# A transformer block on one core: the attention steps, taken apart into units, follow written sequences on all five queues

## The chip, the core and the metric

The kernel runs on one core of a Trainium2 chip. TensorE (PE, with its weight loads shown as PEld), VectorE (DVE), ScalarE (ACT) and GpSimd (POOL) compute; the fifth queue, SyncE (SP), issues the transfers. Each has an instruction queue of its own, which runs in the order in which it was written, and semaphores hold an instruction until its data are there and its buffer is free. The metric is the device time of one execution in microseconds, the median of several runs.

## The reference

One transformer block over 2048 tokens of width 1024, all in float32. `phi` is t + 1 for positive t and exp(t) otherwise.

```python
mod = silu(c) @ w_mod                           # six rows of 1024: sa, ca, ga, sb, cb, gb
h = layernorm(x) * (1 + ca) + sa
# attention: 32 heads of 32, four segments of 512 tokens
for s in range(4):
    p = softmax(qs @ ks.T * scale + mask)       # the mask is -1e9 * (row < col)
    o = g * (phi(qs) @ M) / (phi(qs) @ z + 1e-6) + (1 - g) * (p @ vs)
    M += phi(ks).T @ vs;  z += sum(phi(ks))     # the memory, used by the next segment
x = x + ga * (concat(o) @ wo)
h = layernorm(x) * (1 + cb) + sb
x = x + gb * ((gelu(h @ w_gate) * (h @ w_up)) @ w_down)     # the feed-forward is 3584 wide
```

## The kernel before

**Products.** Almost every product is made of three: each operand is cut into a high part, of the type float32r, and a low part, the rest. ACT or DVE writes the high part (a cast or a copy), DVE or POOL the low one (a subtraction), and PE multiplies high by high, low by high and high by low.

**Stages.** The opening loads x and the conditioning, normalises segments 0 and 1 and projects the first group. Then come 32 attention steps: a step is one group of four heads (there are eight) in one segment; the first sixteen steps are segments 0 and 1 of each group, the others segments 2 and 3. Then the output projection, and the feed-forward, which is most of the time. The change lies in the attention steps alone.

**An attention step.** In the loop's turn n, three steps overlap: the projections of step n+1, the scores of step n and the values of step n−1.

- K and Q: 96 key-value matmuls (128x256, in two PSUM banks, tag `mm`) and 24 query matmuls (128x512). ACT and DVE copy them out (`kn`, `vx`); PE transposes `kn` (`kT`); ACT and DVE cut kT and q into high and low (`kh`, `kl`, `qh`, `ql`), and SP spreads these over the rows of `ks` and `qs`.
- S: for each of four rows of score blocks, four matmuls (one per head) into PSUM banks of the tag `s`, of which there are five. DVE adds the mask and takes the row maximum (`mm`) in one instruction; ACT takes the exponential of the result (`sj`, three buffers) for its sum (`ll`) alone. From `mm` DVE makes `mt`, turns it (`tt`) and writes it into rows 96 to 127 of `qs`, so that the transposed scores come out with the maximum subtracted; from `ll` come `rc` (DVE) and `rx` (ACT).
- T and O: the transposed scores of the step before (`T`, four column blocks, 16 matmuls, again banks of the tag `s`), the exponential on ACT (`pt`), the causal edge on POOL, and the product with `vx` (`O`, 32 small matmuls). T needs the `qs` rows from the step's own maxima.
- A (`sums`) adds to the memory `M`; M (`memory`) makes `mz`, the matmuls `num`, the denominators `dn` and the share `ry`. R and Y transpose the factors `rx` and `ry`, and DVE combines them with O; SP stores the result.

Beside these, each pair of steps loads and cuts the three weights of the next group (POOL subtracts in quarters), steps 1 to 9 normalise segments 2 and 3 (rows `na`: statistics, scale, eight transposes and their scaling, a store to `hT_d`), one or two columns of the conditioning are made in each step by a 1024-wide DVE reduction (`wm`), steps 14 and 15 load `hT_d` back and cut it, and steps 29 to 32 prepare the output projection. Weights, rows of x and conditioning columns share four buffers (tag `raw`).

**What sets the order.** PE's order is written: the string `ORDER` of 30 letters says which generator is advanced next, and `todo` holds the loads and cuts with their positions. The same string serves every step. PE follows the program order. On SP, DVE, ACT and POOL a scheduler places the attention's instructions by its own estimates, a few excepted (`hold`); in the opening and the feed-forward these queues follow the program too.

Of the kernel before, what the change touches and what calls it, by code (L numbers as in the profile page):

```python
# [19 lines left out]
P = 128  # L20
# [16 lines left out]
def block_kernel(ctx: ExitStack, tc: tile.TileContext, x, c, wmod, wq, wkv, wo, beta, wg, wu, wd, out):  # L37
# [149 lines left out]
    def load_hT(src, s, dst, name, late=False):  # L187

        rs = []
        for k in range(KT // 2 + 1):  # L190
            if k < KT // 2:
                r = raw_tile(f"r{name}_{k}").rearrange("p (k t) -> p k t", t=L)
                nc.sync.dma_start(r, src[2 * k * P:(2 * k + 2) * P, s * L:(s + 1) * L].rearrange("(k p) t -> p k t", p=P))
                rs.append(r)
            yield
            for q in range(2 if k > 0 else 0):
                r = rs[k - 1]
                hi = hT_tile(f"hh{name}_{k}_{q}", s)
                lo = hT_tile(f"hl{name}_{k}_{q}", s)
                if late:  # L200
                    nc.scalar.activation(hi, r[:, q], AF.Copy)
                else:
                    nc.vector.tensor_copy(hi, r[:, q])
                (nc.gpsimd if q else nc.vector).tensor_sub(lo, r[:, q], f32(hi))
                dst.append((hi, lo))
                yield
# [20 lines left out]
    def norm_tiles(src, dst, segs, jscale, jshift, name, tiles=range(4), wait=0, get=raw_tile, more=[]):  # L227
# [8 lines left out]
        def stats(q):  # L236
            t = xs[q]
            mv, rs = norm_stats([t[:, :L], t[:, L:]], f"{name}{toks[q]}", name == "a")
            norm_scale([t], mv, rs, f"{name}{toks[q]}")

        def turn(q, h):
# [6 lines left out]
            for k in range(4):  # L248
# [3 lines left out]
                if name == "b" and k % 2:  # L252
# [4 lines left out]
            if wait:  # L257
                later(3, send_h)
            else:
                send_h()  # L260

        if wait:
            for q in range(len(toks)):
# [10 lines left out]
                for h in range(2):  # L274
                    turn(q, h)
                    yield
            return
        if name == "a":
            load(0)
            yield  # L280
            for q in range(len(toks) + 1):
                if q < len(toks):
                    stats(q)
                yield
                for h in range(2):
# [53 lines left out]
    hT, W, Mst, ST, SC, PK = {}, {}, {}, {}, {}, {}  # L339
# [5 lines left out]
    def weights(half, g, at):  # L345

        W[g] = [None] * 3
        raws = [None] * 3

        def get(i):  # L350
            raws[i] = fetch((wq[g], wkv[g, 0], wkv[g, 1])[i], f"{i}_{half}_{g}")

        def cut(i):
            W[g][i] = split_w(raws[i], wsp_tile(f"w{i}_{half}_{g}"))

        for pos, f, i in at:
            todo.append((pos, lambda f=f, i=i: (get, cut)[f](i)))
# [14 lines left out]
    def kv_tiles(n, nm):  # L372
# [3 lines left out]
        ST[n] = [None, ks_t[n % 2], vx, None]  # L376
# [7 lines left out]
    def k_out(n, s, nm, kn, vx):  # L384
        ks = ks_t[n % 2]
        ps = s_ps("kT" + nm)
        for t in range(4):
            nc.tensor.transpose(ps[:, t * P:(t + 1) * P], kn[:, t], ident)  # L388
        kh = t2("kh" + nm, "sp", bufs=4, dt=F32R)
        kl = t2("kl" + nm, "sp", bufs=4, dt=F32R)  # L390
        nc.scalar.activation(kh, ps, AF.Copy)
        nc.vector.tensor_sub(kl, ps, f32(kh))
        for qd, srct in ((0, kh), (1, kh), (2, kl)):
            nc.sync.dma_start(f32(ks[qd:96:3]), f32(srct))
        if s < NSEG - 1:
            knf = kn.rearrange("p a b -> p (a b)")
            e = tmp_tile("ek" + nm)
            nc.scalar.activation(e, knf, AF.Exp)
            nc.vector.tensor_scalar_min(e, e, 1.0)
            pk = t2("pk" + nm, "pk", shape=(P, 4, P))  # L400
            nc.vector.scalar_tensor_tensor(pk.rearrange("p a b -> p (a b)"), knf, 0.0, e, op0=ALU.max, op1=ALU.add)
            PK[n] = pk, vx

    def q_out(n, s, nm, ps):
        qh = t2("qh" + nm, "sp", bufs=4, dt=F32R)
        ql = t2("ql" + nm, "sp" if n else "sj", bufs=4 if n else 3, dt=F32R)
        nc.scalar.activation(qh, ps, AF.Copy, scale=SCALE)
        nc.vector.scalar_tensor_tensor(ql, ps, SCALE, f32(qh), op0=ALU.mult, op1=ALU.subtract)
        qs = t2("qs" + nm, "qs", bufs=2, dt=F32R, shape=(P, 4, L))
        pq = None  # L410
        if s > 0:
            e = tmp_tile("eq" + nm)
            nc.scalar.activation(e, ps, AF.Exp)
            nc.vector.tensor_scalar_min(e, e, 1.0)
            pq = t2("pq" + nm, "pq", bufs=2)
            nc.vector.scalar_tensor_tensor(pq, ps, 0.0, e, op0=ALU.max, op1=ALU.add)
        for qd, srct in ((0, qh), (1, ql), (2, qh)):
            nc.sync.dma_start(f32(qs[qd:96:3]), f32(srct))
        ST[n][0], ST[n][3] = qs, pq

    def kv_part(n, g, s):

        nm = f"{g}_{s}"
        kn, vx = kv_tiles(n, nm)
        for tp in range(2):
            ps = mm_ps(f"kv{nm}_{tp}")
            for t in range(2):
                for kt in range(KT):
                    kv_mm(ps[:, 2 * P * t:2 * P * (t + 1)], g, s, 2 * tp + t, kt)
                    if kt == 3 or (kt == 7 and t == 0):  # L430
                        yield
            kv_out(ps, kn, vx, 2 * tp, 2)
            yield
        k_out(n, s, nm, kn, vx)
        yield

    def q_part(n, g, s):

        nm = f"{g}_{s}"
        ps = mm_ps("q" + nm)  # L440
        for kt in range(KT):
            q_mm(ps, g, s, kt)
            if kt % 2 == 1 and kt < KT - 1:
                yield
        q_out(n, s, nm, ps)
        yield

    def first_part(n, g, s):

        nm = f"{g}_{s}"  # L450
        kn, vx = kv_tiles(n, nm)
        kv = [mm_ps(f"kv{nm}_{tp}") for tp in range(2)]
        psq = o_ps("q" + nm)
        for kt in range(KT):
# [14 lines left out]
        k_out(n, s, nm, kn, vx)  # L469
        q_out(n, s, nm, psq)  # L470
        yield

    def sums(n, g, s):

        nm = f"{g}_{s}"
        if s < NSEG - 1:
            pk, vx = PK.pop(n)
            ps = s_ps("M" + nm)
            for t in range(4):
                nc.tensor.matmul(ps[:, :P + 2], pk[:, t], vx[:, t], start=(t == 0), stop=(t == 3))  # L480
            M = t2("Mt" + nm, "M", bufs=11, shape=(P, P + 2))
            if s == 0:
                nc.vector.tensor_copy(M, ps[:, :P + 2])
            else:
                nc.vector.tensor_add(M, ps[:, :P + 2], Mst[g, s - 1])
            Mst[g, s] = M
        yield

    def scores(n, g, s):
        nm = f"{g}_{s}"  # L490
        qs, ks, vx, pq = ST[n]
        mm = t2("mm" + nm, "mm", bufs=2, shape=(P, 4, 4))
        ll = t2("ll" + nm, "ll", bufs=2, shape=(P, 4, 4))

        for i in range(4):
# [10 lines left out]
            if i < 3:  # L506
                yield

        mt = t2("mt" + nm, "mt", bufs=2, dt=F32R, shape=(P, 4, 4, 2))
        nc.vector.tensor_copy(mt[:, :, :, 0], mm)  # L510
        nc.vector.tensor_sub(mt[:, :, :, 1], mm, f32(mt[:, :, :, 0]))
        tt = t2("tt" + nm, "tt", bufs=1, shape=(P, P))
        mtf = f32(mt.rearrange("p a b c -> p (a b c)"))
        for a in range(4):
            nc.vector.transpose(tt[96:128, 32 * a:32 * a + 32], mtf[32 * a:32 * a + 32])
        for i in range(4):
            nc.vector.tensor_scalar(qs[96:128, :, i * P:(i + 1) * P], tt[96:128].unsqueeze(1).to_broadcast([32, 4, P]),  # L517
                                    seli[96:128, i:i + 1], None, op0=ALU.mult)

        rc = t2("rc" + nm, "rc", bufs=2, shape=(P, 4, 4))  # L520
        nc.vector.reciprocal(rc, ll)
        nc.vector.tensor_mul(rc, rc, omg[:, 4 * g:4 * g + 4].unsqueeze(1).to_broadcast([P, 4, 4]))
        rx = t2("rx" + nm, "rx", shape=(P, 4, 4, DH))
        nc.scalar.activation(rx, rc.unsqueeze(3).to_broadcast([P, 4, 4, DH]), AF.Copy)
        SC[n] = [rx, None]

    def memory(n, g, s):
        nm = f"{g}_{s}"
        pq = ST[n][3]
        if s > 0:  # L530
            M = Mst[g, s - 1]
            mz = t2("mz" + nm, "mz", bufs=1, shape=(P, P + 4))
# [15 lines left out]
            SC[n][1] = ry  # L548
        yield

    def values(n, g, s):
        nm = f"{g}_{s}"
        qs, ks, vx, pq = ST.pop(n)
        rx, ry = SC.pop(n)

        po = o_ps("O" + nm)
        pts = {}
# [13 lines left out]
        def PV(kc):  # L571
            for j in range(4):
                nc.tensor.matmul(po[32 * j:32 * j + 32, kc * P:], vx[:, kc, 32 * j:32 * j + 32], pts[kc, j],  # L573
# [984 lines left out]
```

## Time and profile before

| | |
|---|---|
| median of 3 runs | 2793.05 us (2791.14 to 2793.16) |
| the profiled execution | 2794.09 us |
| its span, first to last instruction | 2792.4 us |
| mean granted TensorE clock | 0.995 |
| PE busy | 2737.9 us, 98% of the span |
| DVE, ACT, POOL busy | 1553.5, 1202.4, 880.2 us |

The profile belongs to one execution. Matmuls are pipelined and overlap in the records, and the end of one is modelled; so PE can look busy while it waits, and the distance from one matmul's start to the next is the safer reading. "Idle before" a group names the instruction that ended the wait.

### The profile page before, as it was taken

To read this page: it belongs to the slowest core of one execution; us is meant where nothing else is said; L and a number is where in the kernel's file an instruction comes from. 1 tells how busy PE (TensorE), PEld (TensorE's weight loads), DVE (VectorE), ACT (ScalarE), POOL (GpSimd) and SP (SyncE) were. 2 spreads that over 40 slices of the span, in tenths; PEclk is the share of its full clock that TensorE was granted. 3 is DMA by queue.
4 is the path that set the end of the run, shared out by engine and by line. 5 is a ranking of instruction groups with operands and counts; after the bars stand their busy time and mean duration, and the time that the engine had idled before them with its cause. 6 is when DMAs were issued, how large, how long until landed. Compare 5 with 4: busy or idle time off the path is not lost.

```text
span 2792.4 us, 43055 instructions
## 1 busy us (share of the span) xinstructions
PE 2737.9 (98%) x14748; PEld 2285.7 (82%) x14748; DVE 1553.5 (56%) x3499; ACT 1202.4 (43%) x2826; POOL 880.2 (32%) x1424
## 2 busy tenths in 40 slices
PE   7999999999999999999999999999999999999999
PEld 6888888888888777778888878888888888888887
DVE  7666566866666735555555445344343245475456
ACT  5777776767676624234332333111111033233323
POOL 5333334433332523245555552535352000000000
PEclk8999999999999999999999999999999999999999
DMA  6455544454434538768898767999999687796563
GB/s 229 138 136 145 148 118 137 137 147 114 125 99 118 153 123 264 260 257 309 309 357 312 279 266 276 344 353 367 353 360 332 225 288 266 261 306 217 177 205 127
DMA packets 244890, 637.77 MB, mean 228 GB/s; under 512 B 24768, under 2 KB 49344, under 8 KB 244672
## 3 DMA queue, kind: packets, MB, share of 16 engines
q1 hardware_dynamic: 244672, 635.03, 67.5%
q8 instruction: 116, 1.90, 0.3%
q14 instruction: 102, 0.84, 0.1%
HBM read 372.79 MB, written 211.81 MB: 209 GB/s over the span
## 4 chain that ended last, share of the span: by engine, by line
PE 84%; DVE 5%; ACT 5%; issue 2%; DMA 2%; POOL 2%; SPq 0%; ACTq 0%; DVEq 0%; POOLq 0%
PE f L1049 36%; PE y L1248 19%; PE kv L364 10%; PE y L633 4%; PE q L370 4%; PE T L564 3%; PE O L573 2%; PE S L500 2%; ACT sj L504 2%; ACT pt L566 1%; POOL w L181 1%; ACT w L176 1%; DVE qs L517 1%; PE num L538 0%; PE M L480 0%
## 5 line engine op out<-in xcount | busy, mean ns | idle before, releaser
L1049 PE MATMUL f<-A,B 128*128 128x512 f32 x4704 | 1075.0, 390 | 3.4 <-DVE c L1069 1.6
L1049 PEld LDWEIGHTS f<-A,B 128*128 128x128 f32 x4704 | 880.8, 188 | 190.7 <-DVE c L1069 2.8
L1248 PE MATMUL y<-B,L 128*128 128x512 f32 x2352 | 533.3, 389 | 0.0
L1248 PEld LDWEIGHTS y<-B,L 128*128 128x128 f32 x2352 | 441.4, 188 | 91.7
L502 DVE CUSTOM_DVE_ANT_0 sj<-S,mask 128x384 f32<-128x384 f32 (+3 forms) x512 | 231.0, 487 | 213.6 <-PE S L500 178.4
L504 ACT ACTIVATE sj<-sj,mm 128x384 f32<-128x384 f32 (+3 forms) x512 | 280.9, 551 | 47.1 <-DVE mm L502 46.6
L567 POOL TENSOR_SCALAR_AFFINE_SELECT pt<-pt 128x128 f32<-128x128 f32 x512 | 164.2, 340 | 347.9 <-ACT pt L566 340.3
L566 ACT ACTIVATE pt<-T 128x256 f32<-128x256 f32 (+3 forms) x512 | 180.7, 456 | 99.2 <-PE T L564 93.4
L763 ACT ACTIVATE L<-X 128x512 fp32r<-128x512 f32 x168 | 105.8, 630 | 256.4 <-PE y L1248 165.8
L364 PE MATMUL kv<-w,hhh 128*128 128x256 f32 x1024 | 201.4, 285 | 0.0
L765 DVE TENSOR_TENSOR L<-X,L 128x512 fp32r<-128x512 f32 x168 | 115.8, 690 | 144.6 <-ACT L L763 144.5
L181 POOL TENSOR_TENSOR w<-r,w 128x256 fp32r<-128x256 f32 x180 | 130.7, 757 | 162.9 <-ACT w L176 152.6
L1072 ACT ACTIVATE g<-g 128x512 f32<-128x512 f32 x56 | 35.3, 631 | 340.0 <-DVE g L1071 340.0
L364 PE MATMUL kv<-w,hha 128*128 128x256 f32 x896 | 175.5, 284 | 0.2 <-DVE vx L382 0.2
L988 POOL TENSOR_TENSOR rw<-rw,gbb 128x256 f32<-128x256 f32 x112 | 92.0, 855 | 247.1 <-DMA rw<-wd 187.2
L364 PEld LDWEIGHTS kv<-w,hhh 128*128 128x128 f32 x1024 | 166.5, 192 | 0.5
L364 PEld LDWEIGHTS kv<-w,hha 128*128 128x128 f32 x896 | 144.9, 191 | 1.2 <-PE kT L388 0.4
L364 PE MATMUL kv<-w,hlh 128*128 128x256 f32 x512 | 145.1, 283 | 0.0
L564 PE MATMUL T<-qs,ks 128*128 128x256 f32 (+2 forms) x512 | 121.3, 346 | 12.1 <-ACT pt L566 6.7
L633 PE MATMUL y<-wo,hho 128*128 128x512 f32 x384 | 128.2, 398 | 1.9 <-DVE xr L637 1.9
L364 PE MATMUL kv<-w,hla 128*128 128x256 f32 x448 | 126.6, 283 | 0.0
L1065 ACT ACTIVATE g<-f 128x512 f32<-128x512 f32 x56 | 33.5, 598 | 207.3 <-PE f L1049 207.3
(242 smaller groups left out, 4213.3 us busy)
## 6 DMA issues: line engine op xcount, KB each, us to landing
bc_d<-B SPq DMA_DIRECT2D x189, 512.0 KB, 5.3
B<-bc_d SPq DMA_DIRECT2D x189, 512.0 KB, 5.5
B<-wc_d SPq DMA_DIRECT2D x112, 512.0 KB, 3.7
hid_d<-g SPq DMA_DIRECT2D x56, 512.0 KB, 4.5
wc_d<-T SPq DMA_DIRECT2D x56, 512.0 KB, 7.3
X<-hid_d SPq DMA_DIRECT2D x112, 256.0 KB, 4.7
wr<-gd_d SPq DMA_DIRECT2D x84, 256.0 KB, 4.1
ks<-kh SPq DMA_DIRECT2D x64, 256.0 KB, 4.5
```

Of the source, the lines that this page charges most:

```text
L181: eng.tensor_sub(w[:, 1, k:k + 256], r[:, k:k + 256], f32(w[:, 0, k:k + 256]))
L364: nc.tensor.matmul(ps, b[:, sl], w[:, a], start=(kt == 0 and a == 0 and b is hi), stop=(kt == KT - 1 and a == 1), **kw)
L370: nc.tensor.matmul(ps, w[:, a], b, start=(kt == 0 and a == 0 and b is hi), stop=(kt == KT - 1 and a == 1), **kw)
L502: nc.vector.tensor_tensor_reduce(out=sj[:, :nv], in0=ps[:, :nv], in1=mask[:, L - nv:], scale=-1.0, scalar=3.4e38, op0=ALU.add, op1=ALU.min ...
L504: nc.scalar.activation(sj[:, :nv], sj[:, :nv], AF.Exp, bias=mm[:, j, i:i + 1], scale=-1.0, accum_out=ll[:, i, j:j + 1])
L564: nc.tensor.matmul(ps[:, :nn], ks[:, j, kc * P:(kc + 1) * P], qs[:, j, L - nn:], start=True, stop=True)
L566: nc.scalar.activation(pt, ps[:, nn - n:nn], AF.Exp)
L567: nc.gpsimd.affine_select(pt[:, :P], pt[:, :P], pattern=[[1, P]], compare_op=ALU.is_ge, fill=0.0, base=0, channel_multiplier=-1)
L633: nc.tensor.matmul(ps, b[:, i * P:(i + 1) * P], w[:, a, g % 2], start=(g == 0 and a == 0 and b is hi), stop=(g == G - 1 and a == 1))
L765: eng.tensor_sub(lo[:, k], src[:, k], f32(hi)[:, k])
L1049: nc.tensor.matmul(ps, B[m, i][:, a, kt * P:(kt + 1) * P], A[p, i, kt][b], start=(start and kt == 0 and a == 0 and b == 0), stop=(kt == 3 ...
L1248: nc.tensor.matmul(banks[t], ops[k][:, y, t * P:(t + 1) * P], B[slots[k]][:, x], start=(i not in (2, 4, 3) and j == 0 and x == 0 and y == ...
```

## The change

The loop with its string and its `todo` list is replaced by `attention()`. Each step's work is cut into some seventy named units, and `ORDER` gives for each kind of step the sequence in which they are written: the step's number or numbers are the key. PE's order thus changes too, and SP, DVE, ACT and POOL follow the same written sequence, without the scheduler. A unit is what one function writes, on whatever engines: `S0` to `S3` the rows of scores, `T0` to `T3` and `P0`, `P2` the values, `K0` to `K7` and `Q0` to `Q3` the projections (12 and 6 matmuls each), `o0`, `o1` their copies, `kt`, `ek`, `dk`, `qo`, `ea`, `eb`, `dq` what follows them, `tm`, `tq`, `tr` the maxima and shares, `A`, `mz`, `nu`, `dn` the memory, `rt`, `rm`, `yt`, `zs` the end of the values, `G`, `C`, `D`, `l`, `L`, `m` the weights' load, high part and low halves, `ns`, `nc`, `n0`, `n1`, `nd`, `ne`, `nl` the norm's statistics, scale, turns, stores and load, `wl`, `wd` the conditioning's load and reduction, `x` a piece of loading, `ga`, `wo`, `wp` the output projection's.

Besides, in the norm the second four scalings of a row go from ACT to DVE; in `load_hT` the high part of every second column goes to ACT and POOL subtracts its low part in two halves; the stores of the first output rows to `x1_d` are put off by two steps. The matmuls are the same.

```diff
-    ORDER = "K N K V K V N K K V N V K V K S Q S V V S K A S Q M K Q Q V V"
-    ORDER0 = "K N K N K N K N K K S K S K S K S A K K M"
+    ORDER = {
+        (0,):
+            "K N K G1 N K N K G2 N G0 K K S0 K S1 C1 K S2 l1 K C2 S3 L1 l2 tm tq A tr L2 K",
+        (1,):
+            "T0 K0 K1 D0 ns K2 T1 rt nc P0 mz m0 nu dn K3 T2 n0 n1 o0 Q0 Q1 T3 nd S0 ne nl m1 P2 S1 rm S2 K4 "
+            "Q2 S3 yt tm Q3 K5 K6 K7 tq wl qo o1 zs tr dq A kt ea eb dk ek",
+        (2, 4, 6, 8):
+            "G1 Q0 T0 wd Q1 T1 Q2 P0 ns nc T2 Q3 T3 qo G2 n0 rt P2 K0 ea eb S0 C1 K1 dq S1 K2 S2 l1 K3 n1 K4 "
+            "nl C2 S3 L1 rm l2 K5 tm G0 wl K6 o0 K7 nd o1 ne tr A tq yt kt dk L2 ek zs",
+        (3, 5, 7):
+            "ns D0 K0 K1 T0 K2 T1 nc m0 K3 wl o0 wd P0 n0 K4 S0 K5 S1 mz Q0 S2 Q1 A S3 nd K6 m1 n1 tm nl Q2 "
+            "tq rt T2 Q3 ne T3 qo ea K7 P2 o1 rm nu dq tr dn yt kt dk eb zs ek",
...
+        (18, 20, 22, 24, 26, 28):
+            "G2 G0 K0 K1 K2 T0 K3 T1 G1 o0 rt P0 T2 Q0 T3 S0 Q1 S1 mz wd Q2 Q3 qo C1 K4 C2 S2 K5 S3 P2 rm l1 "
+            "dq ea yt zs eb K6 K7 A tm nu l2 o1 kt tr ek wl dk tq L1 L2 dn",
+        (19, 21, 23, 25, 27):
+            "mz wd D0 K0 K1 K2 m0 m1 K3 o0 T0 K4 T1 Q0 S0 K5 S1 Q1 rt S2 P0 S3 Q2 T2 tm K6 Q3 T3 wl tq qo K7 "
+            "P2 rm o1 nu ea kt yt tr dq dn dk zs wd ek wl eb",
...
+    def attention(nseg1):
+        load, stat, scale, turn, put = norm_tiles(x, hT_d, (2, 3), 1, 0, "a")
...
+        for n in range(len(steps) + 1):
+            u = {}
+            if n > 0:
+                values(u, n - 1, *steps[n - 1][1:])
+            if n < len(steps):
+                scores(u, n, *steps[n][1:])
...
+            elif n + 1 < len(steps):
+                project_in(u, n + 1, *steps[n + 1][1:])
...
+            for q in next(o for k, o in ORDER.items() if n in k).split():
+                beside(u, q, n)
+        send(True)
+        waiting[0] = False
...
-        free_order[0] = True
...
+        with tc.manual_schedule(engines={E.SP, E.DVE, E.Activation, E.Pool}):
+            attention(nseg1)
```

What this does to the queues, at the two places of which the prediction speaks most. First the beginning of step 1: PE from the memory's matmuls on (M, then the transposes kT, then the projections kv and the first T). Before:

```order
L480 MATMUL M_0_945<-vx_0_306,pk_0_629 128x130 x4
L388 MATMUL kT_1_952<-ident,kn_1_665 128x128 x4
L364 MATMUL kv_0_0_991<-w_0_1_878,hha_0_252 128x256
L364 MATMUL kv_0_0_991<-w_0_1_878,hla_0_253 128x256
...
L364 MATMUL kv_0_0_991<-w_0_1_982,hla_7_544 128x256
L564 MATMUL T_0_00_1028<-qs_0_635,ks_111 128x512
L564 MATMUL T_0_10_1033<-qs_0_635,ks_111 128x512
```

and now:

```order
L566 MATMUL M_0_948<-vx_0_306,pk_0_629 128x130 x4
L401 MATMUL kT_1_962<-ident,kn_1_667 128x128 x4
L615 MATMUL T_0_00_992<-qs_0_635,ks_111 128x512
L615 MATMUL T_0_10_997<-qs_0_635,ks_111 128x512
L615 MATMUL T_0_20_1002<-qs_0_635,ks_111 128x512
L615 MATMUL T_0_30_1007<-qs_0_635,ks_111 128x512
L367 MATMUL kv_0_0_1015<-w_0_1_867,hha_0_252 128x256
```

The 24 kv matmuls that stood between kT and the first T now stand behind it. On DVE, what T waits for (the copies of vx, the memory's copy Mt, the maxima mt, their turn tt, the rows of qs), before:

```order
L382 COPY vx_1_666<-kv_1_1_669 128x2x128
L502 ISA sj_0_33_925,mm_0_806<-S_0_33_923,mask 128x512
L502 ISA mm_0_806 128x1
L483 COPY Mt_0_950<-M_0_945 128x130
L510 CAST mt_0_928<-mm_0_806 128x16
L533 TENSOR_TENSOR mz_1_1340<-Mt_0_950,blk 128x128
L511 TENSOR_TENSOR mt_0_928<-mm_0_806,mt_0_928 128x16
L534 TENSOR_SCALAR mz_1_1340<-sel_106,Mt_0_950 128x4
L515 STREAM_TRANSPOSE tt_0_931<-mt_0_928 32x32 x4
L521 RECIPROCAL rc_0_940<-ll_0_807 128x16
L517 TENSOR_SCALAR qs_0_635<-tt_0_931,seli 32x4x128 x4
```

and now:

```order
L526 ISA sj_0_33_929,mm_0_810<-S_0_33_927,mask 128x512
L526 ISA mm_0_810 128x1
L534 CAST mt_0_936<-mm_0_810 128x16
L535 TENSOR_TENSOR mt_0_936<-mm_0_810,mt_0_936 128x16
L539 STREAM_TRANSPOSE tt_0_939<-mt_0_936 32x32 x4
L543 TENSOR_SCALAR qs_0_635<-tt_0_939,seli 32x4x128 x4
L569 COPY Mt_0_953<-M_0_948 128x130
```

The memory's copy, mz and rc went behind the rows of qs. Second, SP where the weights of a later group are loaded, in step 6 (r are weights, wm a conditioning column, R an output to be stored, na a row of x for the norm). Before:

```order
L155 DMA wm_2978<-wmod 128x1024
L111 DMA r_0_4_3180<-wkv 128x1024
L598 DMA oT_d<-R_0_2970 128x512
L111 DMA r_0_4_3239<-wkv 128x1024
L394 DMA ks_111<-kh_0_3086 32x4x512 x2
L394 DMA ks_111<-kl_0_3087 32x4x512
```

and now:

```order
L654 DMA oT_d<-R_0_3021 128x512
L111 DMA r_0_4_3143<-wkv 128x1024
L111 DMA r_0_4_3278<-wkv 128x1024
L390 DMA qs_1_3277<-qh_1_3271 32x4x512 x2
L390 DMA qs_1_3277<-ql_1_3272 32x4x512
L238 DMA na_3452<-x 128x1024
L111 DMA r_0_4_3501<-wq 128x1024
```

The two key-value weights now stand side by side behind the store; before, the store stood between them.

More of the change, by code (lines that the diff above doesn't have):

```diff
@@ L382, in kv_out, with spread, after_kv @@
         nc.vector.tensor_copy(vx[:, t:t + n, :P], psv[:, :, P:])
-    def k_out(n, s, nm, kn, vx):
+    def spread(dst, parts):
+        for row, part in parts:
+            nc.sync.dma_start(f32(dst[row:96:3]), f32(part))
+    def after_kv(u, n, s, nm, get):
         ks = ks_t[n % 2]
[L386 to L402, printed above, removed]
@@ L437, in q_part, with turned @@
[L437 to L446, printed above, removed]
+        tiles = {}
+        def turned():
+            kn = get()[0]
+            ps = s_ps("kT" + nm)
+            for t in range(4):
+                nc.tensor.transpose(ps[:, t * P:(t + 1) * P], kn[:, t], ident)
+            kh = tiles["h"] = t2("kh" + nm, "sp", bufs=4, dt=F32R)
+            kl = tiles["l"] = t2("kl" + nm, "sp", bufs=4, dt=F32R)
+            nc.scalar.activation(kh, ps, AF.Copy)
+            nc.vector.tensor_sub(kl, ps, f32(kh))
@@ L525, in scores, with maxima @@
[L525 to L530, printed above, removed]
+        def maxima():
+            mm = d["mm"]
+            mt = t2("mt" + nm, "mt", bufs=2, dt=F32R, shape=(P, 4, 4, 2))
+            nc.vector.tensor_copy(mt[:, :, :, 0], mm)
+            nc.vector.tensor_sub(mt[:, :, :, 1], mm, f32(mt[:, :, :, 0]))
+            tt = d["tt"] = t2("tt" + nm, "tt", bufs=1, shape=(P, P))
+            mtf = f32(mt.rearrange("p a b c -> p (a b c)"))
+            for a in range(4):
+                nc.vector.transpose(tt[96:128, 32 * a:32 * a + 32], mtf[32 * a:32 * a + 32])
```

440 lines of the change are left out of this document (259 added, 181 removed).

## The prediction

> **What bounds the kernel now.** I read the shares of the page first, then the stages, then pairs of attention steps.
>
> The page's busy line, and its chain of waits:
>
> ```profile
> PE 2737.9 (98%) x14748; PEld 2285.7 (82%) x14748; DVE 1553.5 (56%) x3499; ACT 1202.4 (43%) x2826; POOL 880.2 (32%) x1424
> ...
> PE 84%; DVE 5%; ACT 5%; issue 2%; DMA 2%; POOL 2%; SPq 0%; ACTq 0%; DVEq 0%; POOLq 0%
> ```
>
> TensorE sets the end. A shorter time must come from its waits, and the change removes no matmul. Now the stages (columns: stretch, its length, then busy us and instructions of PE, PEld, DVE, ACT, POOL, then granted clock, DMA share, GB/s):
>
> ```profile
> 95.50:997.20 901.70, 885.21 (x6417) 758.47 (x6420) 608.10 (x2002) 639.24 (x1844) 324.04 (x736) 1.00 0.47 130
> ...
> 1172.00:2255.00 1083.00, 1078.18 (x4771) 888.39 (x4771) 497.24 (x709) 278.40 (x493) 454.00 (x556) 1.00 0.85 311
> ```
>
> The change leaves the feed-forward alone (the second row is its first part, with 4.8 us of idle PE). It acts on the first row, the attention steps 1 to 31, and on a few us at either side. Cut at the first O matmul of a step, that row is:
>
> ```profile
> 95.50:155.40 59.90, 58.76 (x429) 49.84 (x431) 38.94 (x129) 44.54 (x124) 20.71 (x48) 1.00 0.48 120
> 155.40:275.40 120.00, 118.03 (x861) 101.02 (x864) 78.39 (x258) 92.87 (x265) 39.10 (x97) 1.00 0.52 142
> 275.40:337.90 62.50, 59.52 (x432) 50.54 (x435) 38.67 (x125) 47.71 (x138) 21.76 (x52) 1.00 0.51 138
> 337.90:395.40 57.50, 56.22 (x421) 48.71 (x424) 35.45 (x120) 41.20 (x119) 21.85 (x50) 1.00 0.51 142
> 395.40:450.20 54.80, 54.80 (x417) 48.25 (x420) 33.37 (x119) 37.65 (x112) 12.82 (x38) 1.00 0.38 104
> 450.20:568.00 117.80, 114.65 (x836) 97.44 (x838) 87.99 (x274) 77.93 (x228) 51.15 (x100) 1.00 0.52 152
> 568.00:681.20 113.20, 111.55 (x837) 97.21 (x840) 77.04 (x269) 80.28 (x230) 43.12 (x100) 1.00 0.49 131
> 681.20:848.70 167.50, 167.35 (x1252) 145.78 (x1256) 110.56 (x381) 116.77 (x342) 55.39 (x138) 1.00 0.41 115
> 848.70:903.90 55.20, 55.20 (x421) 48.70 (x423) 35.15 (x127) 37.29 (x112) 12.63 (x38) 1.00 0.37 104
> 903.90:997.20 93.30, 89.14 (x553) 71.00 (x556) 72.56 (x202) 63.00 (x176) 45.49 (x76) 0.98 0.47 139
> ```
>
> Two pairs of steps, 54.80 and 55.20 us, have PE busy to the last tenth. They are the **floor** that the trace itself shows: the first for the first half of the steps, the second for the later half, which has one numerator group and one Y transpose more and one M group less. Steps 1 to 8 also transpose the normalised rows, in groups of four:
>
> ```profile
> 303.49 0.66 PE tpa L247 x4
> ...
> 308.95 0.59 PE tpa L247 x4
> ```
>
> That is 0.63 us a group, so 1.9 us for three groups in a pair and 2.5 for four.
>
> **The room.** Row by row, length less floor: 59.9 − 56.7 = 3.2; 120.0 − 114.6 = 5.4; 62.5 − 57.3 = 5.2; 57.5 − 56.7 = 0.8; then 0; 117.8 − 110.5 = 7.3 (the second of its pairs is given 0.9 more for one more numerator group); 113.2 − 110.4 = 2.8; 167.5 − 165.6 = 1.9; 0; and 93.3 − 82.7 = 10.6 (three steps, 1.5 pairs). In the last step two more waits stand:
>
> ```profile
> 997.14 3.30 PE L573 MATMUL O<-pt,vx 128*32 128x512 f32 x16
> ...
> 1007.62 0.41 PE L573 MATMUL O<-pt,vx 128*32 128x128 f32 x2 [1.16 <-POOL pt L567]
> ```
>
> The same 16 O matmuls take 1.64 us elsewhere (row below), so 1.6 + 1.2 = 2.8. In all **40 us**: 14.6 in steps 1 to 8, 12.0 in the middle, 13.4 at the end.
>
> ```profile
> 681.20 1.64 PE O L573 x16
> ```
>
> How this room is read matters. Span less PE busy gives only 901.7 − 885.2 = 16.5 us. The weight loads give another answer: they fill 758.47 of 901.70 us, 84.1%, against 48.25 of 54.80, 88.0%, in the dense pair; 901.7 × (1 − 84.1/88.0) = 40. [...]
>
> **What makes the room now.** At one of the longest stalls, SP and ACT show it (SP's sequencer first):
>
> ```profile
> 288.04 0.33 SPq L598 DMA_DIRECT2D oT_d<-R  x1
> 293.53 0.33 SPq L111 DMA_DIRECT2D r<-wkv  x1
> ...
> 299.43 1.06 ACT L176 ACTIVATE w<-r 128x1024 fp32r<-128x1024 f32 x1 [4.99 <-DMA r<-wkv]
> 300.39 0.61 ACT L524 ACTIVATE rx<-rc 128x512 f32<-128x512 f32 x1
> ...
> 304.89 1.24 ACT L225 ACTIVATE na<-na,mra,rsa 128x1024 f32<-128x1024 f32 x1 [1.46 <-DVE mra L223]
> ```
>
> A weight load stands in SP's queue behind an output store that is itself late. ACT's queue has the weight's cut at its head and stands still for 5 us, then for 1.5 us more at the norm scale. The exponentials that T needs are behind both. The whole stage:
>
> ```profile
> ACT rx L524 <- DVE rc L522: 52.9, 28, 4.0
> ...
> ACT w L176 <- DMA r<-wkv: 19.7, 6, 5.0
> ...
> ACT na L225 <- DVE mra L223: 10.4, 8, 2.0
> ```
>
> **The change, part by part.** (1) *Loads.* G1 and G2 open an even step, side by side on SP, and their cuts C1 and C2 come behind S0 and S2: at least ten units of PE, some 12 us, against the 5 us lost above. I count the 19.7 us of ACT waiting as gone. (2) *Norm.* The statistics (ns) and the scale (nc) are parted by T0 to T1 in odd steps; in even steps they are still adjacent, so part of the 1.46 us waits stays, on DVE instead of ACT. (3) *S rows.* The written order puts a K unit of 12 matmuls between S rows in steps 2 to 8. One K unit is 1.44 us:
>
> ```profile
> 683.51 1.44 PE kv L364 x12
> ...
> L504 ACT ACTIVATE sj<-sj,mm 128x512 f32<-128x512 f32 x124 | 87.9, 713 | 0.5
> L504 ACT ACTIVATE sj<-sj,mm 128x384 f32<-128x384 f32 x124 | 74.5, 604 | 0.0
> ```
>
> Four exponentials take 4 × 604 ns = 2.4 us for S2 and 2.9 for S3; between these two PE has K3, a group of transposes and K4, 1.4 + 0.6 + 1.4 = 3.4. ACT keeps up, and the banks come free in time. (4) *Moved work.* Half of the norm's transposed scalings (32 of 64, 378 ns by the row below) go from ACT to DVE, 1.5 us in each of eight steps; eight casts of the hT load in steps 14 and 15 go from DVE to ACT, 8 × 0.62 = 5.0 us off a DVE that is busy 88.0 of 117.8. Both land on engines with at least 7 us free in a step, so 0. (5) *POOL's halves* of a 512-wide subtraction, 2 × 757 ns against 1416: 0.1 us each, under DVE and PE work, 0.
>
> ```profile
> L255 ACT ACTIVATE hta<-tpa,modT 128x128 f32<-128x128 f32 x64 | 24.2, 469 | 5.1 <-PE tpa L247 5.1
> ...
> L203 DVE CAST hhh<-rh 128x512 fp32r<-128x512 f32 x16 | 9.7, 619 | 0.0
> ...
> L204 POOL TENSOR_TENSOR hlh<-rh,hhh 128x512 fp32r<-128x512 f32 x8 | 11.3, 1416 | 3.2 <-DVE hhh L203 2.8 <-issue 0.4
> ...
> L181 POOL TENSOR_TENSOR w<-r,w 128x256 fp32r<-128x256 f32 x180 | 130.7, 757 | 162.9 <-ACT w L176 152.6 <-PE S L500 6.7 <-DVE mm L502 3.5
> ```
>
> (6) *The first step loses.* T0 now follows kT at once; before, 24 kv matmuls lay between.
>
> ```profile
> 88.91 1.19 PE L564 MATMUL T<-qs,ks 128*128 128x512 f32 x4 [1.40 <-DVE qs L517]
> ...
> 85.13 0.29 DVE L483 COPY Mt<-M 128x130 f32<-128x130 f32 x1
> ...
> 87.17 1.69 DVE L517 TENSOR_SCALAR qs<-tt,seli 32x512 fp32r<-32x512 f32 x4
> ```
>
> DVE is clear of S at 85.13 and now makes mt, tt and qs without the M copy, mz and rc between them: qs ends near 88.2 instead of 88.9. But kT is done at 84.2, so PE stands still for 4.0 us where it stood for 1.4 with 2.9 us of kv done. Net loss 2 us. A stall of this kind has a second price:
>
> ```profile
> 55.00:60.00 5.00, 2.43 (x20) 2.19 (x19) 4.90 (x9) 3.85 (x7) 1.59 (x2) 0.99 0.55 149
> 60.00:65.00 5.00, 5.00 (x27) 4.56 (x27) 2.29 (x5) 0.78 (x1) 2.96 (x4) 0.67 0.83 169
> ```
>
> After 2.6 us of idleness the clock was 0.67 for 5 us: 1.7 us lost. I take 3 us in all for step 1, between 2 (no throttle) and 5 (throttle, and P0 late too). [...]
>
> **The sum.** Left over after the change: the first pair 3.2 + 3 = 6.2; for the 26 steps between, 0.3 us each (what the regular pairs at 681 to 848 show: 1.9 us in six steps), 8; at the end 4 of 13.4, since DVE has 72.6 us of work in what would be 82.7 us. That is 18 of 40, a gain of **22 us**. Bounds: 40 if all reaches the floor (and step 1 costs nothing), 0 if 1.25 us a step stays. The profiled execution took 2794.09 us, 1.0 over the median; 2794 − 22 = 2772 for it, 2771 for the median. I say **2771**.
>
> **The rivals.** (a) *Only idle PE can be won.* If busy PE hides nothing, the room is 16.5 + 2.8 = 19.3 us, less the 3 and 8 above: 8 won, 2785. For it: 98% busy. Against it: the two dense pairs. (b) *The stalls move.* In a written queue one late unit delays all behind it; if four fifths of the 26.6 us in steps 1 to 28 come back elsewhere and the end keeps its 13.4, 5 us are won: 2788. For it: in steps 3 to 6 ACT is busy 77% and DVE 65% of the time, in bursts. (c) *Slower: late work ahead of T0.* The tr unit has a fixed place before kt and ek; ACT waits there for DVE's rc, and behind it stand kh, ek and T0's exponentials. The present price is 52.9/28 = 1.9 us a wait. If T0 or its exponentials were late by that in each of 30 steps, 57 us are added to a floor 40 below: 2810. It decides from 40/32 = 1.25 us a step on. Against it, in step 2, as counted from row means:
>
> ```profile
> L502 DVE CUSTOM_DVE_ANT_0 sj<-S,mask 128x512 f32<-128x512 f32 x128 | 84.2, 685 | 7.1 <-ACT sj L504 4.3 <-PE S L500 0.7
> ```
>
> After S3, DVE owes four such reductions (2.7), the R product, tm, two copies of vx, rc and M (some 3.5 together by their means) and qs (1.7), 7.9 us; PE has K5, K6, K7, K0, K1 (7.2) and M, Y, kT (some 1.8) ahead of the next T0, 9.0 us. T0 has 1 us to spare: enough, though little. (d) *Nothing moves*: the late half is dense already, and the early half is bound by data that come no sooner in another order: 2793. For it: the pair at 395 shows that the old order can be dense. Against it: the same pair shows that data can be in time.
>
> **How the numbers follow.** Forecast 0.60 (2753 to 2781); (a) 0.16; (b) and (d) together 0.11, on either side of where a gain begins to show; (c) 0.13. A difference under 0.2%, 5.6 us, cannot be told from none. Faster: 0.60 + 0.16 + 0.02 of (b) = 0.78; same: the other 0.09, and 0.01 of a mild (c); slower 0.12. The range from 2753 to 2791 takes in (a) and (b), and leaves out (c) and a little at the low end.
>
> **What would show it.** Right: the cut of the second key-value weight no longer waits for its load; pairs in steps 3 to 8 take 57 to 58 us; the three regular pairs stay at 55 to 56; the first T waits about 4 us for qs; the last three steps take 86 us instead of 93. Wrong: T's wait for pt or qs in most steps, ACT standing at rx, or the pairs at 681 to 848 growing past 57 us; then rival (c) has it.

## The result, and the profile after

The changed kernel takes 2774.22 us (median of 4 runs, 2772.03 to 2775.41); beside it the kernel before took 2792.10 us (2790.61 to 2793.16). The ratio is 0.9935, 95% interval 0.9918 to 0.9953: 17.9 us faster, where 22 were forecast. The profiled execution took 2774.08 us (20.0 less than before), its span is 2772.4 us. The busy line and the chain of waits of the page:

```profile
PE 2725.8 (98%) x14748; PEld 2286.4 (82%) x14748; DVE 1568.4 (57%) x3519; ACT 1204.0 (43%) x2806; POOL 888.9 (32%) x1448
...
PE 89%; DVE 4%; issue 2%; POOL 2%; DMA 1%; ACT 1%; SPq 0%; POOLq 0%; ACTq 0%; DVEq 0%
```

PE's part of the chain grew from 84% to 89%, ACT's fell from 5% to 1%. The stages, cut at the same O matmuls as before (columns as there), then the feed-forward's stretch:

```profile
98.67:157.59 58.92, 58.82 (x438) 51.46 (x437) 39.88 (x135) 45.29 (x128) 19.28 (x49) 1.00 0.55 159
157.59:270.72 113.13, 113.13 (x857) 100.23 (x857) 82.55 (x274) 89.03 (x249) 41.54 (x97) 1.00 0.53 150
270.72:327.30 56.58, 56.58 (x429) 50.12 (x429) 40.56 (x134) 44.38 (x124) 23.24 (x53) 1.00 0.48 132
...
671.12:838.87 167.75, 167.75 (x1249) 146.18 (x1248) 116.98 (x391) 118.34 (x343) 56.54 (x138) 1.00 0.44 123
...
891.54:977.85 86.31, 83.59 (x540) 68.52 (x539) 62.70 (x186) 60.91 (x169) 39.42 (x78) 0.98 0.46 137
98.67:977.85 879.18, 875.79 (x6432) 761.03 (x6431) 615.05 (x2020) 639.30 (x1825) 329.73 (x753) 1.00 0.46 133
1172.00:2255.00 1083.00, 1078.06 (x4771) 888.32 (x4770) 501.25 (x713) 280.05 (x496) 445.16 (x546) 1.00 0.86 314
```

The whole stretch of steps 1 to 31 fell from 901.70 to 879.18 us, although 24 key-value matmuls came into it from the start. Steps 3 to 6 fell from 120.00 to 113.13, steps 7 and 8 from 62.50 to 56.58; the regular pairs (167.50, now 167.75) and the feed-forward did not move. Weight loads now fill 761.03/879.18 = 86.6% of the stretch, before 84.1%, in the dense pair 88.0%.

Steps are cut differently now (some projections moved to a neighbour), so I also take, for every matmul, the distance to the next one's start less the usual distance of its kind (the 30th percentile in the kernel before; for O a mean). The sum over a stretch is time lost by PE, in us, whatever stands in it. "Start" is the first M matmul to the first O; "last" runs from the O of step 32 to the first feed-forward matmul. Where a kernel is told below by its place, it is by this table:

| kernel | start | 1–8 | 9–12 | 13–16 | 17–27 | 28–31 | last |
|---|---|---|---|---|---|---|---|
| before | 3.2 | 20.0 | 3.9 | 9.0 | 9.0 | 12.6 | 14.1 |
| changed | 8.5 | 4.9 | 2.0 | 5.6 | 7.9 | 10.2 | 12.4 |
| old order, written queues | 13.3 | 90.4 | 32.1 | 42.2 | 123.5 | 69.7 | 15.6 |
| new order, scheduler | 11.0 | 25.2 | 6.1 | 8.6 | 8.9 | 9.5 | 9.1 |
| POOL alone by scheduler | 8.7 | 6.8 | 3.8 | 7.4 | 8.0 | 9.1 | 17.2 |
| S rows together | 9.7 | 26.3 | 2.0 | 5.6 | 8.0 | 10.5 | 12.5 |
| load twice | 8.7 | 8.8 | 2.0 | 5.6 | 7.8 | 10.2 | 12.4 |
| three operations back | 8.8 | 8.5 | 2.0 | 11.4 | 7.8 | 11.2 | 11.9 |
| halves back | 9.8 | 4.8 | 2.0 | 8.1 | 7.8 | 12.0 | 12.8 |
| T0 later | 6.5 | 6.5 | 2.0 | 5.6 | 8.0 | 11.5 | 15.3 |
| end mended | 9.7 | 4.9 | 2.0 | 5.6 | 8.0 | 8.3 | 9.5 |
| both | 6.5 | 6.5 | 2.0 | 5.6 | 8.0 | 8.0 | 9.8 |

The change won 15.1 in steps 1 to 8, 5.3 in 9 to 16, 1.1 in 17 to 27, 4.1 at the end, and lost 5.3 at the start: 20.3, as much as the 20.0 us between the two profiled executions.

### The profile page after: what moved, and what is told of

Same layout as the page of the kernel before. It is cut to its first block, busy times and chain, and to the rows that moved or that the text cites. A ratio compares the mean times of both kernels' runs of the same rounds, so it can differ in the third digit from the quotient of the medians.

```text
span 2772.4 us, 43014 instructions
## 1 busy us (share of the span) xinstructions
PE 2725.8 (98%) x14748; PEld 2286.4 (82%) x14748; DVE 1568.4 (57%) x3519; ACT 1204.0 (43%) x2806; POOL 888.9 (32%) x1448
## 4 chain that ended last, share of the span: by engine, by line
PE 89%; DVE 4%; issue 2%; POOL 2%; DMA 1%; ACT 1%; SPq 0%; POOLq 0%; ACTq 0%; DVEq 0%
PE f L1107 35%; PE y L1306 19%; PE kv L367 12%; PE q L373 6%; PE y L690 4%; PE S L524 3%; PE T L615 3%; PE O L627 3%; PE num L583 1%; PE M L566 1%; PE tpb L250 0%; POOL t L827 0%; PE R L633 0%; PE kT L401 0%; PE kv L496 0%
## 5 line engine op out<-in xcount | busy, mean ns | idle before, releaser
L615 PE MATMUL T<-qs,ks 128*128 128x256 f32 (+2 forms) x512 | 108.3, 334 | 7.5 <-DVE qs L543 4.6
```

The source lines that it names most:

```text
L615: nc.tensor.matmul(ps[:, :nn], ks[:, j, kc * P:(kc + 1) * P], qs[:, j, L - nn:], start=True, stop=True)
```

## The experiments

Each is compared with the kernel before, run beside it; differences to the changed kernel are differences of medians. The kernel before took 2792.1 to 2794.5 us beside the different runs, so a difference of some 2 us between medians decides nothing by itself. The table is finer: where an edit touches nothing, its rows agree to 0.2 us in steps 1 to 27, but they differ by 1 us at the start and by up to 3 us from step 28 on.

**The order alone, and the written queues alone.** The new order with the scheduler on the other queues:

```diff
-        with tc.manual_schedule(engines={E.SP, E.DVE, E.Activation, E.Pool}):
-            attention(nseg1)
+        free_order[0] = True
+        attention(nseg1)
```

> The changed kernel with its sequence of units, PE still in that sequence, but with the scheduler placing the instructions of SP, DVE, ACT and POOL in the attention, as in the kernel before. Theory (the gain is the new order of units, which moves stalls out of steps 1 to 16 on PE): most of the gain stays, 2774 to 2784. Rival (the gain is that the queues are written rather than scheduled): it goes, 2788 to 2800.

Measured 2801.31 us, ratio 1.0028 (1.0016 to 1.0039): slower than before. And the old order of 30 letters, written out for all queues (the old loop inside the `manual_schedule` of the changed kernel):

> The kernel before with its old string of 30 letters, but SP, DVE, ACT and POOL follow the program in the attention too, without the scheduler. Theory (order of units): nothing is won; the old generators write long pieces at once, so that late work stands ahead of urgent work: 2793 to 2830. Rival (written queues are the gain): under 2783.

Measured 3110.88 us, ratio 1.1142 (1.1126 to 1.1159). PE's longest sums of waits in the attention part (us in total, times, longest), with the scheduler:

```profile
PE T L615 <- DVE qs L543: 7.9, 1, 7.9
PE O L627 <- POOL pt L618: 6.4, 9, 1.2
```

and with the old order:

```profile
PE num L538 <- DVE mz L534: 161.7, 24, 9.0
```

The old pieces were long: the memory's numerators stand in one piece behind work that DVE does late, and in the written queue PE waited 161.7 us for it (row above). So neither half of the change wins anything; the gain needs the new order in small units and the written queues together (the size of the units and their order were not parted). My expectation that the order by itself carries the gain fell.

**Which queue.** POOL alone is given back to the scheduler (`E.Pool` left out of the set).

> Against the changed kernel, POOL alone is again left to the scheduler in the attention part; SP, DVE and ACT keep their written sequences and PE its new order. With all four left to the scheduler the time was 2801, 27 us over the changed kernel, and there PE waited 6.4 us in nine places for masks that POOL had put behind cuts of weights. If POOL's order is the cause, the time comes near 2790 or above with O waiting for pt again; if DVE's or ACT's order is, it stays within 3 us of 2774. I expect about 2782.

Measured 2782.73 us, ratio 0.9958 (0.9944 to 0.9973): 8.5 of the 27 us, at O in steps 1, 11 and 13 and in the last step. What the scheduler costs on DVE, ACT and SP was not taken apart further.

**The spacing of the S rows.**

```diff
-            "... K0 ea eb S0 C1 K1 dq S1 K2 S2 l1 K3 n1 K4 nl C2 S3 L1 rm l2 K5 tm ..."
+            "... K0 ea eb S0 C1 dq S1 S2 l1 n1 nl C2 S3 K1 K2 K3 K4 L1 rm l2 K5 tm ..."
```

> Against the changed kernel, in steps 2, 4, 6 and 8 the four S rows follow each other with no kT units between them (K1 to K4 come behind S3). By my prediction the spaced rows are what lets the exponentials (ACT) keep up with the sums; without them PE waits for a free score buffer in each of the four steps: 3 to 4 us each, 12 to 16 us in all, about 2788 (2784 to 2792), seen as waits of PE's S rows or of the K units behind them in steps 2 to 8 and nowhere else. The rival: the spacing was worth nothing, PE's later K units only change places, within 2 us of 2774.

Measured 2796.09 us, ratio 1.0007 (0.9998 to 1.0017): all of the gain is gone, 21.9 us, and all of it in steps 1 to 8 (26.3 against 4.9). PE in step 4:

```profile
197.67 3.27 PE L524 MATMUL S<-ks,qs 96*128 96x256 f32 x12
201.94 0.66 PE L250 MATMUL tpa<-ident,na 128*128 128x128 f32 x4 [1.00 <-DVE mm L526]
202.56 2.39 PE L524 MATMUL S<-ks,qs 96*128 96x512 f32 x4
204.74 0.41 PE L367 MATMUL kv<-w,hha 128*128 128x256 f32 x1
```

and the same time in windows of 5 us:

```profile
200.00:205.00 5.00, 4.00 (x13) 2.37 (x13) 3.90 (x18) 5.00 (x16) 2.79 (x4) 0.76 0.34 106
205.00:210.00 5.00, 5.00 (x27) 5.00 (x27) 4.89 (x17) 4.08 (x11) 2.82 (x4) 0.55 0.95 298
210.00:215.00 5.00, 5.00 (x44) 5.00 (x44) 0.50 (x2) 0.39 (x1) 0.00 (x0) 1.00 0.04 11
```

ACT is full (5.00 of 5.00) and PE waits for it, as the theory said, by way of DVE: its maxima, for which PE waits, wait 1.0 us at this place for one of ACT's three `sj`. By the distances of the matmuls such waits are some 3 of the 6.1 us that this step lost. The rest is the clock: the 5 us behind the thin stretch have 27 matmuls, the next 44, and the granted clock was 0.76 and 0.55, so 0.24 × 5 + 0.45 × 5 = 3.4 us at most. That is why 3 to 4 us a step was too little.

**The price of a late load.** First the load one place ahead of its cut (`G2` from behind `qo` to behind `nl`, in steps 2, 4, 6 and 8):

> Against the changed kernel, in steps 2, 4, 6 and 8 the load of the next pair's second key-value weight is issued directly ahead of its cut instead of half a step earlier. Each load took about 4.9 us from issue to landing, so ACT will wait some 3 to 5 us at the head of its queue in each of the four steps, with the exponentials of S3 behind the cut. By my prediction's first term such a wait reaches PE: 2 to 4 us each, 8 to 16 us in all, about 2786. The rival: ACT has room for it (it was 43% busy) and the next instructions of ACT that PE needs are not late: within 2 us of 2774.

Measured 2776.11 us, ratio 0.9939 (0.9924 to 0.9954). It decided nothing: SP is so far ahead of ACT that the load, issued 10 us later, still landed in time, and ACT waited for no load. Steps 1 to 8 took no longer; in the profiled run O of the last step waited 3.2 us for POOL's mask, 1.8 in the changed kernel. So the same load was made twice, one after the other:

```diff
             raws[i] = fetch(src[i], f"{i}_{half}_{g}")
+            if i == 2 and half == 0 and g in (2, 3, 4, 5):
+                nc.sync.dma_start(raws[i], src[i])
```

> As in the run with the load issued directly ahead of its cut, which made ACT wait for nothing (SP ran some 7 us ahead of ACT, so the load had landed), but in steps 2, 4, 6 and 8 the same load is made twice, the second waiting for the first to land: the cut then waits some 2.5 to 4 us at the head of ACT's queue in each of the four steps, about what ACT waited for weights in the kernel before (18.7 us in five). By my prediction's first term such a wait reaches PE: 1.5 to 3 us a step, 2780 to 2788. The rival: the new order has its T units so placed that ACT can be that late, and the time stays within 2 us of the 2776 of the single late load.

Measured 2778.46 us, ratio 0.9947 (0.9933 to 0.9961; its runs spread from 2775.73 to 2781.03). ACT at one of the four places:

```profile
201.77 1.06 ACT L354 ACTIVATE w<-r 128x1024 fp32r<-128x1024 f32 x1 [2.85 <-DMA r<-wkv]
```

and the sum over steps 1 to 8:

```profile
ACT w L354 <- DMA r<-wkv: 7.0, 4, 2.9
```

7.0 us of waiting on ACT cost 8.8 − 4.9 = 3.9 us in these steps: 0.56 us of PE for each us of ACT. If that rate held in the old order too, the 18.7 us that the kernel before waited there are an estimated 10 of the 15.1 us won; no run shows this share directly. The waits in this run were 7 us instead of the 10 to 16 expected, so the cost came out below its range, though the wait does reach PE.

**The moved operations**, all three undone:

```diff
-                if late or q:
+                if late:
...
-                if q:
-                    for c in (slice(0, L // 2), slice(L // 2, L)):
-                        nc.gpsimd.tensor_sub(lo[:, c], r[:, q, c], f32(hi[:, c]))
-                else:
-                    nc.vector.tensor_sub(lo, r[:, q], f32(hi))
+                (nc.gpsimd if q else nc.vector).tensor_sub(lo, r[:, q], f32(hi))
...
-                if h if name == "a" else k % 2:
+                if name == "b" and k % 2:
```

> The changed kernel with the three moved operations put back: all of the norm's scalings on ACT, the high parts of the hT load on DVE, POOL's low part in one piece. Theory: they lie under PE's work, within 3 us of 2774. Rival (the relief of ACT in steps 2 to 9 and of DVE in steps 14 and 15 is what wins): 2780 or more, with T or O waiting in steps 2 to 9 or 14 to 15.

Measured 2784.04 us, ratio 0.9969 (0.9956 to 0.9981): 9.8 us. By place, 3.6 in steps 1 to 8, where only the norm's scalings differ, and 5.8 in 13 to 16, where the hidden rows are loaded. In steps 1 to 8, 1.5 of the 3.6 is seen as a wait of T for these scalings:

```profile
PE T L611 <- ACT hta L254: 1.5, 3, 0.5
```

To part the latter, the two halves on POOL alone were undone:

> Against the changed kernel, only one of the three moved operations is undone: POOL's subtraction of the low halves in the loads of hidden rows is again one instruction of 512 columns instead of two of 256. All three undone cost 9.8 us, of which 5.8 us in steps 13 to 16, where these loads stand: there O waited 2.5 us for a mask of POOL, kv 1.2 us and T 1.1 us. If POOL's longer instruction ahead of the mask is the cause, this run costs 2.5 us or more in steps 13 to 16 (2777 to 2780); the rival is that the cast that went from DVE to ACT is the cause of all of it, and this run stays within 1.5 us of 2774.

Measured 2776.76 us, ratio 0.9939 (0.9922 to 0.9956): 2.5 us over the changed kernel, which between these medians says little; in the table steps 13 to 16 are 2.5 longer (8.1 against 5.6 in every run that leaves them alone), but not at a mask. DVE, POOL and PE at the border of steps 14 and 15 with the halves undone, then DVE and POOL of the changed kernel at the same place:

```profile
486.84 1.01 DVE L203 CAST hhh<-rh 128x512 fp32r<-128x512 f32 x1
487.88 1.73 DVE L204 TENSOR_TENSOR hlh<-rh,hhh 128x512 fp32r<-128x512 f32 x1
...
487.80 1.27 POOL L204 TENSOR_TENSOR hlh<-rh,hhh 128x512 fp32r<-128x512 f32 x1 [0.24 <-ACT hhh L201]
...
490.27 1.35 PE L611 MATMUL T<-qs,ks 128*128 128x384 f32 x4 [1.35 <-DVE kl L401]
```

```profile
487.61 0.42 DVE L203 CAST hhh<-rh 128x512 fp32r<-128x512 f32 x1
488.07 1.11 DVE L208 TENSOR_TENSOR hlh<-rh,hhh 128x512 fp32r<-128x512 f32 x1
...
488.58 2.13 POOL L206 TENSOR_TENSOR hlh<-rh,hhh 128x256 fp32r<-128x256 f32 x2
```

DVE's subtraction takes 0.69 us elsewhere (the median of its eight in this run); beside POOL's it took 1.73, and ended when POOL had been done for 0.5. T stood behind kl, which stood behind that subtraction, and waited 1.35 us, 0.16 in the changed kernel: 1.2 of the 2.5 us. The clock behind it is the rest: from 490.7 to 494.1 us the granted clock was 0.51, in the changed kernel 1.00, which is worth up to 3.4 × 0.49 = 1.7 us. Of the 1.2 us the uncut instruction shows only half (1.73 against 1.11). The other half is the cast ahead of it (1.01 against 0.42), and the two traces differ in which engine began first: with the halves undone the cast began at 486.84, 0.02 us after POOL's last quarter of a weight; in the changed kernel at 487.61, 0.01 us before it, and there POOL's quarter was the longer one, 1.01 us instead of 0.74. So putting the long instruction back cost these steps 2.5 us, by another road than I had expected, and part of it, by these rows, by such a coincidence. DVE's subtraction took 1.73 − 0.69 = 1.04 us longer, where 1.19 were left of POOL's 1.27, which had begun 0.08 us before.

**T0 behind K0 and K1 in step 1.**

> The changed kernel with one place moved: in step 1 the units K0 and K1 come before T0, as in the kernel before. Theory: the 4.6 us in which PE waits for qs there are filled with 2.9 us of kv matmuls, and the granted clock, 0.71 and 0.61 in the ten microseconds around that wait, stays nearer to 1, which is worth some 1.5 us: 2774 - 4.5 = 2770, and the wait of T for qs falls from 4.6 to under 2. Rival: step 1 is bound by the exponentials on ACT behind T0, which come no sooner; the matmuls moved ahead only make a new wait before O: 2774.

Measured 2775.69 us, ratio 0.9938 (0.9923 to 0.9953): nothing won. T's wait fell from 4.6 to 1.8 us and the start from 8.5 to 6.5, but the first steps lost 1.6 again (O waited 0.9 us for POOL). The rest was lost in the last step: O waited 2.9 us for POOL's mask (1.8 to 3.2 in all kernels that have this wait), and behind it the granted clock was 0.50 from 990.3 to 993.7 us.

**The end mended.** In step 30 `tr` goes ahead of the cuts of the output weights, and the second cut moves to step 31; in step 32 `T3` goes ahead of `Q1`.

```diff
-            "... dq o1 x rt wp rm yt kt wp wd dk nu x ea eb tr dn A x ek zs",
+            "... dq o1 x rt tr wp rm yt kt wd dk nu x ea eb dn A x ek zs",
...
-            "mz K0 Q0 T0 T1 rt x P0 T2 ..."
+            "mz K0 Q0 T0 T1 rt x wp P0 T2 ..."
...
-            "K0 K1 Q0 K2 T0 K3 T1 rt P0 T2 Q1 T3 K4 ..."
+            "K0 K1 Q0 K2 T0 K3 T1 rt P0 T2 T3 Q1 K4 ..."
```

The reason, in the changed kernel: DVE, ACT and PE at the end of step 30, and PE in step 32.

```profile
938.41 1.47 DVE L675 TENSOR_TENSOR ro<-ro,gab 128x1024 f32<-128x1024 f32 x1
...
941.40 0.24 DVE L549 RECIPROCAL rc<-ll 128x16 f32<-128x16 f32 x1
...
939.92 1.06 ACT L176 ACTIVATE wo<-ro 128x1024 fp32r<-128x1024 f32 x1 [2.14 <-DVE ro L675]
...
942.09 0.63 ACT L552 ACTIVATE rx<-rc 128x512 f32<-128x512 f32 x1 [1.11 <-DVE rc L550]
...
943.26 2.08 PE L615 MATMUL T<-qs,ks 128*128 128x512 f32 x6 [2.65 <-ACT pt L617]
...
988.95 1.14 PE L627 MATMUL O<-pt,vx 128*32 128x128 f32 x8 [1.81 <-POOL pt L618]
```

> Against the changed kernel, two orders at the end are mended: in step 30 tr goes ahead of the two cuts of output weights (the second of them moves into step 31, behind T1), and in step 32 T3 goes ahead of Q1. My reading of the changed trace: the first T of step 31 waits 2.7 us because the chain to its exponentials stands behind those cuts on DVE and ACT, and O of step 32 waits 1.8 us for the mask of its T on POOL behind a cut of 4.0 us. Expected 2770 (2768 to 2772), with both waits gone. The rival: the cut moved into step 31 makes something else late and the time stays within 1.5 us of 2774.

Measured 2770.67 us, ratio 0.9919 (0.9902 to 0.9935), 3.5 us better than the changed kernel. Both waits are gone; what is left of the first is 0.55 us.

**Both, as a version.** Mended end and T0 later:

> The two mended orders at the end (2770.7 alone) together with T0 behind K0 and K1 in step 1 (no difference alone, but 2 us earlier at the first O of step 9, lost again at O of step 32, where that order is now mended): 2768.5 (2767 to 2770). The rival: T0's place is worth nothing, 2770 to 2771.

Measured 2768.75 us (5 runs, 2768.08 to 2769.69), ratio 0.9912 (0.9899 to 0.9926). With the cut `C2` of step 0 behind `S3` besides:

> The same with the cut of the second key-value weight of step 0 behind S3 instead of ahead of it, so that the exponentials of S3 and with them the sums and kT of step 1 come about 1 us earlier: 2767.5 (2766 to 2769), the wait of kT for mm gone. The rival: K0 of step 1 waits for that weight's low half on POOL and takes it back, 2769 to 2772.

Measured 2768.60 us (2768.47 to 2768.96), ratio 0.9912 (0.9898 to 0.9926): no difference. kT's wait for mm stayed at 1.8 us, and kv took the time, nearly as the rival said: it waited 1.8 us for the weight's high part on ACT and 0.6 for a low part on POOL. These two are the fastest found, some 5.5 us under the changed kernel. What T0's place gives in them isn't settled: from the first M to the O of step 9 the profiled runs took 244.5 us with it, 244.8 in the changed kernel and 246.1 with the end alone mended. The 2 us that I had read off the earlier run were an opening that happened to end 1.8 us sooner.

## Why the prediction was right, point by point, and where it was not

**Right in sign and near in size:** 2774.2 against 2771, inside the likeliest case's own range. That the size is so near is partly luck. By the sum's own rows (its 14.6 takes in steps 9 and 10, which gained 2.1; its end begins with step 29, and step 28 lost 1.5) the table's distances give 11.9 us up to step 10 with the start, where the sum had 6.0 (14.6 less 3.2, 3 and eight steps at 0.3); 2.8 in steps 11 to 28, where it had 6.6; and 5.6 from there on, where it had 9.4. The errors, +5.9, −3.8 and −3.8, nearly cancel. Nor is the middle's gain the order's: with the three moved operations undone, steps 13 to 16 lose 11.4 us, more than the 9.0 of the kernel before.

**The room and its reading: right.** Rival (a), that only idle PE can be won, would have had 16.5 us to draw on. The stretch became 22.5 us shorter, and PE's busy time in it fell from 885.21 to 875.79 with no matmul removed; 9.4 us of busy PE had been waiting. The regular pairs stayed at 55.9 us, as said. One row was misread: steps 9 and 10 hold one group of the norm's transposes (four `tpa`), not three, so their room is 57.5 − 55.4 = 2.1 instead of 0.8, and the whole 41 instead of 40.

**(1) Loads and (3) S rows: right in kind.** No weight's cut waits for its load any more, pairs in steps 3 to 8 take 56.6 us, a little less than the 57 to 58 said, and the two experiments price the steps: 0.56 us for each us that ACT waits, 5.4 us a step for rows without spacing. The latter isn't a gain over the kernel before, whose S rows had other work between them too; it is what the new order would have lost otherwise.

**(2) Norm: half right.** Part of the waits stayed, as said, but on ACT and not on DVE: ACT's norm scale waits 4.6 us in four places, 10.4 in eight before.

**(4) Moved work "so 0" and (5) halves "0": wrong.** Without them 9.8 of the 17.9 us are lost. The step that failed is "both land on engines with at least 7 us free in a step": a mean over a step does not say whether the engine is free where PE waits. In steps 2 to 8 T units stood behind ACT's scalings, and the halves matter by DVE's subtraction beside POOL's (1.73 us uncut and 1.11 cut, 0.69 elsewhere), not for their own length. The casts, which leave 3.3 of the 5.8 us in steps 13 to 16, were not undone alone.

**(6) Step 1: too small, 3 said, 5.3 measured**, a little over its upper bound of 5. T waited 4.6 us (4.0 said). What the sum left out is a second wait ahead of it: kT stood 1.8 us for mm, where it had stood 0.2 (for kn). PE in the changed kernel, then DVE:

```profile
85.42 0.63 PE L401 MATMUL kT<-ident,kn 128*128 128x128 f32 x4 [1.78 <-DVE mm L526]
90.66 2.07 PE L615 MATMUL T<-qs,ks 128*128 128x512 f32 x4 [4.61 <-DVE qs L543]
```

```profile
83.91 0.76 DVE L385 COPY vx<-kv 128x256 f32<-128x256 f32 x2 [1.49 <-ACT kn L384]
...
86.41 0.68 DVE L526 CUSTOM_DVE_ANT_0 sj<-S,mask 128x512 f32<-128x512 f32 x1
87.02 0.08 DVE L526 DVE_READ_ACCUMULATOR2_ANT mm<- 128x1 f32 x1
...
88.91 1.69 DVE L543 TENSOR_SCALAR qs<-tt,seli 32x512 fp32r<-32x512 f32 x4
```

"DVE is clear of S at 85.13" was read from the old order and no longer held. In the new one the copies of vx stand ahead of the last row's four reductions and wait 1.5 us for ACT; DVE is clear of S at 87.10, and qs ends at 90.60 instead of 88.2. The windows around the waits:

```profile
85.00:90.00 5.00, 0.63 (x4) 0.42 (x4) 4.82 (x17) 3.02 (x9) 2.78 (x4) 0.71 0.00 0
90.00:95.00 5.00, 4.34 (x20) 3.96 (x21) 3.69 (x10) 3.54 (x8) 0.29 (x1) 0.61 0.25 75
```

In the second window 0.39 × 4.34 = 1.7 us are lost with PE at work, as much as I had read from the earlier stall. The clock also makes this loss uncertain: the table's other five rows that begin step 1 in the same order have 8.7 to 9.8 at the start, the higher ones (9.7 and 9.8) where the clock was at 0.50 for 10.2 us, the lower ones where it was for 6.8.

**The end: mis-sized, 9.4 said, 5.6 measured** from step 29 on (4.1 with step 28). "At the end 4 of 13.4" argued from DVE's sum, 72.6 us of work in 82.7, not from its order. In one place rival (c) was true: tr behind two cuts; in another a cut on POOL. Mending both gave 3.5 us. The line "the last three steps take 86 us" came out at 86.31 for the wrong reason: the step ahead of them grew from 28.0 to 32.8 us, since projections moved there.

**The rivals.** (b) did not come true: the stalls of steps 1 to 16 did not come back later. (c) held in one step of 31: ACT waits at rx as long as before, but T hardly ever stands behind it.

```profile
ACT rx L552 <- DVE rc L550: 49.0, 32, 4.6
```

The two runs with half of the change show that (b) and (c) were no idle fears: 2801 and 3111.

## What to carry to other kernels

Written queues paid here only with units so small and so ordered that little that is late stands ahead of what the bounding engine needs next; the same written queues with the old long pieces cost 11%. When work is moved to an engine with time to spare, ask what stands behind it at that place, and what takes longer beside it (DVE's subtraction 1.73 us instead of 0.69): here operations costed at nothing were worth half of the gain. And a stall of PE has to be priced with the clock behind it: in step 4 of the run with the S rows together some 3 us of waits stood beside up to 3.4 us of lower clock.

## What the runs showed of the hardware

The clock fell here without a long idle stretch of PE: the longest before either fall below was 1.78 us. With the S rows together PE waited once for 1.0 us by the records and had 13 matmuls in 5 us; the granted clock was 0.76 in these and 0.55 in the next 5. In finer windows it was 1.00 until 202.6 us and 0.50 from there to 209.4, and from 199.2 to 202.6 us PE was busy for 2.32 with 9 matmuls. In step 1 of the changed kernel it was 1.00 from 83.7 to 87.1 us and 0.50 from 87.1 to 93.9, so it fell when T's wait of 4.6 us was 1.05 us old; ahead of that wait PE had worked 0.63 us, at kT, behind its wait of 1.78. In both cases thin work was enough.

DVE and POOL took longer beside each other, in these rows the one that began second. The same DVE subtraction of 512 columns took 0.69 us alone; 1.11 in the changed kernel, where it began while POOL was at the last quarter of a weight; and 1.73 where it began 0.08 us behind POOL's uncut subtraction. DVE's cast that began 0.01 us ahead of such a quarter kept its 0.42 us, and POOL's quarter took 1.01 instead of 0.74.
